# Batch 0's second MLP layer in seven products, with the weight sums made in its first layer

## The chip, the cores and the metric

The kernel runs on 1 core of one Trainium2 chip. The metric is the device time of one execution in microseconds (us); the number given for a kernel is the median of its runs. The engines are TensorE (PE; its weight loads are listed as PEld), VectorE (DVE), ScalarE (ACT), GpSimd (POOL) and the queue SyncE (SP), on which nearly all loads and stores are issued. Each engine works through its own instructions in order. A difference under about 1% can't be told from no change with the runs used here.

## The reference

Retention (a linear attention with decay) feeds a mixer with a low-rank step over the tokens and an MLP over the channels:

```python
state = gamma * state + k[t] ⊗ v[t];  x[t] = scale * q[t] @ state      # 4 batches, 8 heads, 768 tokens, 64 wide
u  = x + ((x.T @ U) @ V).T                                             # U 768x32, V 32x768
ch = np.maximum(u @ w_ch1, 0.0) @ w_ch2                                # w_ch1 512x2048, w_ch2 2048x512
out = u + ch                                                           # (4, 768, 512), float32
```

## The kernel before, in words

All matrix products run in bfloat16, with sums in PSUM in float32. Tokens are cut into 6 chunks of 128. The program is a list of slots: `weave(main, side)` walks over the main slots of a batch and, ahead of slot i, puts out the work that `put(side, i, f)` has filed there. What is left over for slots past the last one comes at the end, with no main work between. The text of the program thus fixes the order on every engine; an engine never leaves its own order, and waits only for data and for buffers.

A batch b takes two stages, and the attention of batch b+1 is filed as side work in them:

* **First MLP layer** (`mlp1`, `mlp1_two`): 32 slots, one for each of 16 blocks m of 128 hidden channels and each half hf of the tokens (384). A slot is 4 matmuls `bk<-uT,w1b` of 384 columns, and a Relu by ACT or DVE (`evict`) into `gT`. `n1` = 32 is the first slot of the second layer.
* **Second MLP layer**. Batch 0 uses `mlp2`: 48 slots, each 2 matmuls `bk<-w2b,gT` of 512 columns; the first slot of a token chunk also makes `Vb @ Ps` (the low-rank part of `u`) in the same PSUM bank, and the last adds `x` on DVE and stores the chunk. Batches 1 to 3 use `product`: `gT` and `w2b` are cut in quarters and seven quarter products (named "4", "5", "1", "2", "3", "7", "6" in the order in which they run) give what eight would. That is 3 token chunk pairs x 7 products x 2 halves = 42 slots of 4 matmuls of 256 columns. `after` adds each product to the result: ACT copies some products out of PSUM (`s`, `c`), POOL adds those copies, DVE adds others straight from PSUM. The low-rank part is then made apart, by `mix_r`, ahead of the products: a matmul of 512 columns and a DVE add into `res`.

The seven products need sums of quarters. `g_sums(b, n)` makes those of `gT` on DVE, five instructions of 768 elements for each of four groups n; it is filed in the first layer where its blocks are done, the last group at slot n1. `w2_sum(i)` makes those of `w2b` on DVE: three into `w2s`, two in place into `w2b`, each of 2048 elements in a partition. Batches 1 to 3 use the same sums, and before the change they are made once, in batch 1's first layer, at slots 5, 8, 11, 14 and 17.

The side work of one chunk of the next batch's attention: `ret_in` (POOL makes `kd` and `qd` from the loaded float32 chunks), `ret_T` (PE turns them into a bank, ACT or DVE copies them out as `qkT`; from batch 2 on by DMA), `ret_S` (the scores, 64-row matmuls, and two DVE instructions that mask them into `a`), `ret_O` (output, running sum and state). After the last chunk come `mix_P`, `mix_n` and `mix_u`, which make `uT` for the next first layer. `at`, `S_at`, `O_at` and `lead` hold the slots.

w1 comes in six loads and w2 in four, all issued by POOL within the first 30 us; a load of w2 holds four blocks m. `w2_quads` cuts w2 into b11, b12 (blocks 0 to 7, left and right) and b21, b22 (blocks 8 to 15).

Of the kernel before, what the change touches and what calls it, by code (L numbers as in the profile page):

```python
# [47 lines left out]
def kernel(  # L48
# [58 lines left out]
    def mm_bank(who="main"):  # L107
        if use[who] is None:
            who = "main"
        b = use[who][n_use[who] % len(use[who])]  # L110
        n_use[who] += 1
        taken[b] = n_bank[0]
        return bank(b)

    def matmul(o, l, r, cols, **kw):
        nc.tensor.matmul(o, l, r, **kw)  # L116
        bal.mm(cols)
# [407 lines left out]
    def res_of(b, j):  # L525
        if (b, j) not in res:
            res[b, j] = resp.tile([P, DM], fp32, tag="res", name=f"res_{b}_{j}")
        return res[b, j]
# [32 lines left out]
        for m, o in zip(ms, g):  # L561
            evict(gTs[b][:, m, ts(hf, HS)], o, HS, relu=True)

    chp = {}

    def mlp2(b, j, part, of):

        if part == 0:
            chp[b, j] = mm_bank()
            matmul(chp[b, j], Vb[:, ts(j, P)], Ps[b], DM, start=True, stop=False)  # L570
        ch = chp[b, j]
        for m in range(part * NM // of, (part + 1) * NM // of):
            matmul(ch, gTs[b][:, m, ts(j, P)], w2b[:, m], DM, start=False, stop=(m == NM - 1))
        if part == of - 1:
            o = res_of(b, j)
            nc.vector.tensor_tensor(o, chp.pop((b, j)), xs[b, j], op=ALU.add)
            bal.book("V", 0.69)
            nc.sync.dma_start(out=out[b, ts(j, P)], in_=o)
# [6 lines left out]
    def w2_quads():  # L585
        left, right = ds(0, HN), ds(HN, HN)
        return w2b[:, lo, left], w2b[:, lo, right], w2b[:, hi, left], w2b[:, hi, right]

    def w2_sum(i):
        b11, b12, b21, b22 = w2_quads()  # L590
        o, x, y, op = ((w2s[:, 0], b11, b22, ALU.add), (w2s[:, 1], b11, b12, ALU.add),
                       (w2s[:, 2], b21, b22, ALU.add), (b12, b12, b22, ALU.subtract),
                       (b21, b21, b11, ALU.subtract))[i]
        nc.vector.tensor_tensor(o, x, y, op=op)
        bal.book("V", 1.2)

    gss = {}

# [108 lines left out]
    def mlp2_slots(b, of=8):  # L707
        if b == 0:
            return [lambda j=j, i=i: mlp2(b, j, i, of) for j in range(NCK) for i in range(of)]
# [17 lines left out]
    def put(side, i, f):  # L727
        side.setdefault(int(i), []).append(f)
# [52 lines left out]
    for f, *args in (  # L781
# [10 lines left out]
        (qd, 2, 0, V), (turn_q, 2, 1), (keep, 3, 0), (load_w1, 0, 256), (load_w1, 256, 256),  # L792
# [13 lines left out]
        (evict_u, 1, 3, A), (evict_u, 1, 2, V), (load_w1, 512, 256),  # L806
        (load_w1, 768, 256),
    ):
        f(*args)

# [1 line left out]
    for b in range(B):  # L812
        nxt = b + 1 < B
        slots = mlp1_slots(b)
        n1 = len(slots)
        side = {}
        set_banks([0, 1, 2, SA, SB, OB])
        if b == 0:
            taken.update({i: n for n, i in enumerate((1, 2, 0, OB, SA, SB, TP))})
            set_banks([1, 2, 0, OB, SA, SB, TP])  # L820
            slots[:4] = [lambda: mlp1_two(0, (0, 1), 0), lambda: None,
                         lambda: mlp1_two(0, (0, 1), 1), lambda: None]
            for i, s in ((1, 2), (2, 3)):
                put(side, i, lambda s=s: load_w1(512 * s, 512))
            for s in range(4):
                put(side, 4 + s, lambda s=s: load_w2(s))
            for c, nm in ((0, "kq"), (1, "kq"), (2, "kq"), (0, "v"), (3, "kq"), (1, "v"), (4, "kq"),
                          (2, "v"), (3, "v"), (5, "kq"), (4, "v"), (5, "v")):
                put(side, 14, lambda c=c, nm=nm: load_chunk(1, c, nm))
            at, lead, mix_at = [n1 + 7 + 5 * c for c in range(NCK)], 4, n1 + 38  # L830
            S_at = {(0, 1): n1 + 14, (2, 3): n1 + 24, (4,): n1 + 30, (5,): n1 + 35}
            O_at = [n1 + i for i in (19, 22, 29, 32, 35, 38)]
        if b == 1:
            slots[:2] = [lambda: mlp1_two(1, (0, HM), 0), lambda: None]
            for j in range(NCK):
                if not by_token(1, j):
                    put(side, 6 + 3 * j, lambda j=j: mix_r(1, j))
            for i in range(5):
                put(side, 5 + 3 * i, lambda i=i: w2_sum(i))
        if b:  # L840
            for n, i in enumerate((13, 17, 25, n1)):
                put(side, i, lambda n=n: g_sums(b, n))
            banks = [0, 1, 2, TP] if nxt else [0, 1, 2, TP, SA, SB, OB, ST]
            put(side, n1, lambda: free_from(banks))
        if b and nxt:
            set_banks([0, 1, 2])
            at, lead, mix_at = [10 + 4 * c for c in range(NCK)], 5, n1 + 21
            S_at = {(0, 1): 27, (2,): 36, (3,): 40, (4,): 44, (5,): 48}
            O_at = [31, 34, 41, 45, 49, 53]
        if nxt:  # L850
            ret_side(b + 1, at, lead, S_at, O_at, side)
            if b == 0:
                put(side, n1, lambda: set_banks([0, 1], [2]))
            put(side, mix_at, lambda: use.update(mix=[2, SA, SB, OB] if b == 0 else [SA, SB, OB]))
# [35 lines left out]
```

## Time and profile before

| | us |
|---|---|
| median of 3 runs | 226.21 |
| lowest, highest | 225.68, 227.8 |
| the profiled execution | 227.9 |
| its span in the profile | 226.1 |
| PE busy in the span | 215.3 |
| DVE, ACT, POOL busy | 127.8, 124.3, 92.4 |

A row of the timeline gives start and length in us, engine, line, operation, output<-inputs, shapes and how many instructions were merged; in brackets the idle time ahead of it and what ended that. A row of the windows gives, for each engine, busy time and number of instructions in a stretch, then the granted clock of TensorE (1.00 is full), and the DMA's share and rate. A row on a tile gives shortest, median and longest duration in ns.

### The profile page before, as it was taken

What the parts mean: (1) busy time and instruction counts of PE and PEld (TensorE: products, weight loads), DVE (VectorE), ACT (ScalarE), POOL (GpSimd) and SP (SyncE); (2) the same over time, 40 slices, a digit from 0 to 9 for tenths busy, and PEclk for the clock granted to TensorE, in tenths of its full rate; (3) what the DMA queues carried; (4) which work ended last, traced back from release to release, by engine and by line L of the source; (5) the groups of instructions that cost most, each with busy time, mean ns of one, the idle gap of its engine ahead of it and who ended that gap; (6) DMA issues with size and microseconds to landing.
All of it is one profiled execution on the core that took longest, in us unless ns stands there. A gap on an engine that the chain in (4) does not pass through costs nothing.

```text
span 226.1 us, 4887 instructions
## 1 busy us (share of the span) xinstructions
PE 215.3 (95%) x1927; PEld 144.5 (64%) x1927; DVE 127.8 (57%) x249; ACT 124.3 (55%) x256; POOL 92.4 (41%) x110
## 2 busy tenths in 40 slices
PE   7998999999999999994999999999999999999991
PEld 2466656655656465652788776557887865568881
DVE  8497630003777466999884831668983632555213
ACT  3377757751355376764356546777544747772220
POOL 6856920047643512641143279513606230006550
PEclk9999999999999999998899999999999999999999
DMA  6998999999999999996599268979630651000222
GB/s 172 244 263 176 167 182 205 197 215 229 203 251 233 229 202 216 181 183 93 111 231 236 83 142 209 209 132 173 73 117 2 162 94 71 0 3 0 93 97 93
DMA packets 100774, 34.89 MB, mean 154 GB/s; under 512 B 87152, under 2 KB 97808, under 8 KB 100752
## 3 DMA queue, kind: packets, MB, share of 16 engines
q1 hardware_dynamic: 94640, 30.29, 66.0%
q0 software_dynamic: 6112, 4.29, 12.9%
q8 instruction: 15, 0.25, 0.5%
q14 instruction: 7, 0.06, 0.1%
HBM read 27.46 MB, written 6.29 MB: 149 GB/s over the span
## 4 chain that ended last, share of the span: by engine, by line
PE 66%; issue 11%; SPq 7%; POOL 7%; DMA 5%; DVE 1%; ACT 1%; POOLq 0%; DVEq 0%; ACTq 0%
PE bk L116 64%; DMA v_n<-in_v_dram 3%; POOL res L661 3%; POOL s L661 3%; SPq L136 2%; SPq L166 2%; SPq L288 2%; DMA q_n<-in_q_dram 2%; PE bk L424 1%; DVE res L661 1%; POOL qd L262 1%; ACT st L299 1%; POOL kd L257 0%; POOLq L885 0%; ACT kT L299 0%
## 5 line engine op out<-in xcount | busy, mean ns | idle before, releaser
L116 PE MATMUL bk<-uT,w1b 128*128 128x384 bf16 x512 | 85.9, 328 | 0.4 <-DVE res L661 0.4
L121 ACT ACTIVATE gT<-bk 128x384 bf16<-128x384 f32 x124 | 60.6, 490 | 30.2 <-PE bk L116 30.2
L116 PEld LDWEIGHTS <-w1b 128*128 128x128 bf16 x512 | 50.0, 98 | 33.6 <-issue 1.2
L116 PEld LDWEIGHTS <-gT 128*128 128x128 bf16 x392 | 36.9, 99 | 14.3 <-issue 1.2
L116 PE MATMUL bk<-w2b,gT 128*128 128x256 bf16 (+1 forms) x240 | 44.6, 319 | 0.0
L661 POOL TENSOR_TENSOR s<-s,s 128x256 f32<-128x256 f32 x18 | 13.1, 729 | 65.0 <-ACT s L657 65.0
L257 POOL TENSOR_TENSOR kd<-k_n,Gk 128x512 bf16<-128x512 f32 x18 | 20.1, 1117 | 47.5 <-ACT gT L121 18.9
L608 DVE TENSOR_TENSOR gs<-gT 128x768 bf16<-128x768 bf16 x36 | 22.9, 674 | 21.6 <-ACT gT L121 21.3
L446 DVE TENSOR_TENSOR a<-bk,mask 128x512 bf16<-128x512 f32 x36 | 22.8, 684 | 4.5 <-PE bk L116 4.4
L661 DVE TENSOR_TENSOR res<-bk,res 128x256 f32<-128x256 f32 x28 | 10.8, 420 | 21.6 <-PE bk L116 17.1
L116 PEld LDWEIGHTS <-gs 128*128 128x128 bf16 x216 | 20.5, 98 | 3.0
L262 POOL TENSOR_TENSOR qd<-q_n,Gq 128x512 bf16<-128x512 f32 x18 | 19.9, 1105 | 6.2 <-DMA qkT<-qd 3.8
L116 PE MATMUL bk<-w2b,gs 128*128 128x256 bf16 x144 | 19.7, 273 | 0.0
L463 ACT ACTIVATE x<-bk 128x512 bf16<-128x512 f32 x18 | 10.7, 595 | 15.0 <-PE bk L116 13.1
L116 PE MATMUL bk<-w2s,gT 128*128 128x256 bf16 (+1 forms) x152 | 18.5, 267 | 0.0
L657 ACT ACTIVATE s<-bk 128x256 f32<-128x256 f32 x27 | 10.1, 381 | 15.2 <-PE bk L116 14.9
L125 DVE COPY qkT<-bk 128x1024 bf16<-128x1024 bf16 x3 | 2.1, 692 | 23.9 <-PE bk L424 23.9
L268 ACT ACTIVATE vb<-v_n 128x512 bf16<-128x512 f32 x18 | 11.2, 623 | 5.8 <-DMA v_n<-in_v_dram 5.8
L661 POOL TENSOR_TENSOR res<-res,s 128x256 f32<-128x256 f32 x18 | 13.0, 724 | 1.4
L533 DVE TENSOR_TENSOR res<-bk,x 128x512 f32<-128x512 f32 x18 | 11.6, 685 | 3.4 <-PE bk L116 3.4
L116 PE MATMUL bk<-vb,a 128*128 128x64 bf16 (+1 forms) x208 | 10.3, 195 | 3.1 <-DVE a L446 3.1
L538 ACT ACTIVATE x<-res 128x512 bf16<-128x512 f32 x15 | 9.1, 627 | 6.3 <-DVE res L533 6.2
(99 smaller groups left out, 234.5 us busy)
## 6 DMA issues: line engine op xcount, KB each, us to landing
out_dram<-res SPq DMA_DIRECT2D x23, 256.0 KB, 2.4
k_n<-in_k_dram SPq DMA_DIRECT2D x22, 256.0 KB, 5.0
v_n<-in_v_dram SPq DMA_DIRECT2D x22, 256.0 KB, 4.8
q_n<-in_q_dram SPq DMA_DIRECT2D x18, 256.0 KB, 5.1
w2b<-in_moe_w_ch_dram POOLq DMA_DIRECT2D x4, 512.0 KB, 15.2
in<-in_q_dram SPq DMA_DIRECT2D x3, 512.0 KB, 6.3
w1b<-in_moe_w_ch_dram POOLq DMA_DIRECT2D x4, 256.0 KB, 5.7
w1b<-in_moe_w_ch_dram POOLq DMA_DIRECT2D x2, 512.0 KB, 9.1
```

The lines of the kernel that those rows point to most:

```text
L116: nc.tensor.matmul(o, l, r, **kw)
L121: nc.scalar.activation(o, i, AF.Relu if relu else AF.Copy)
L257: eng.tensor_tensor(kd, k_n, Gk[:, c].unsqueeze(2).to_broadcast([P, H, D]), op=ALU.mult)
L262: eng.tensor_tensor(qd, rc[b, c]["q_n"], Gq[:, c].unsqueeze(2).to_broadcast([P, H, D]), op=ALU.mult)
L268: nc.scalar.activation(vb, rc[b, c]["v_n"], AF.Copy)
L446: nc.vector.tensor_tensor(r["a"][:, e], r["s"][e].rearrange("p (n t) -> p n t", n=NP), mask4, op=ALU.mult)
L463: nc.scalar.activation(x_of(b, c), o, AF.Copy)
L533: nc.vector.tensor_tensor(res_of(b, j), h, xs[b, j], op=ALU.add)
L538: nc.scalar.activation(xs[b, j], res[b, j], AF.Copy)
L608: nc.vector.tensor_tensor(o, x, y, op=op)
L657: nc.scalar.activation(t[nm], o, AF.Copy)
L661: eng.tensor_tensor(o, x, y, op=op)
```

## The change

Batch 0 uses the seven products too. So `mlp2` goes; `mix_r` makes batch 0's low-rank part in its first layer (slots 4, 6, 13, 15, 21, 23); `g_sums` runs for batch 0 as well (slots 9, 17, 25 and n1). The sums of w2 move from batch 1's first layer to batch 0's and are cut in two halves h (four blocks m of each side, 1024 elements): the five of half 0 are filed at slot 19 and go to POOL, those of half 1 at slot n1-2, four on DVE and one on POOL. For the halves to be there, w1 and w2 are loaded in pairs of blocks (first of the upper and the lower half, then the next), and batch 0's first layer takes its blocks in the order 0, 1, 8, 9, 2, 3, 10, 11 and so on. Batch 1's scores come one chunk at a time, with new slots for its attention; its last pieces (`mix_n`, `mix_u`) get slots 41 to 47 behind n1, where the last main slot is n1+41. The PSUM banks of batch 0's second layer are 0, 1, 2 for the products.

```diff
-    def w2_sum(i):
-        b11, b12, b21, b22 = w2_quads()
-        o, x, y, op = ((w2s[:, 0], b11, b22, ALU.add), (w2s[:, 1], b11, b12, ALU.add),
-                       (w2s[:, 2], b21, b22, ALU.add), (b12, b12, b22, ALU.subtract),
-                       (b21, b21, b11, ALU.subtract))[i]
-        nc.vector.tensor_tensor(o, x, y, op=op)
-        bal.book("V", 1.2)
+    def w2_sum(i, h, eng):
+        b11, b12, b21, b22 = (x[:, ts(h, HM // 2)] for x in w2_quads())
+        z = w2s[:, :, ts(h, HM // 2)]
+        o, x, y, op = ((z[:, 2], b21, b22, ALU.add), (b21, b21, b11, ALU.subtract),
+                       (z[:, 0], b11, b22, ALU.add), (z[:, 1], b11, b12, ALU.add),
+                       (b12, b12, b22, ALU.subtract))[i]
+        eng.tensor_tensor(o, x, y, op=op)
...
         if b == 0:
-            return [lambda m=m, hf=hf: mlp1(b, m, hf) for m in range(NM) for hf in (0, 1)]
+            ms = [m + x for m in range(0, HM, 2) for x in (0, 1, HM, HM + 1)]
+            return [lambda m=m, hf=hf: mlp1(b, m, hf) for m in ms for hf in (0, 1)]
...
-            at, lead, mix_at = [n1 + 7 + 5 * c for c in range(NCK)], 4, n1 + 38
-            S_at = {(0, 1): n1 + 14, (2, 3): n1 + 24, (4,): n1 + 30, (5,): n1 + 35}
-            O_at = [n1 + i for i in (19, 22, 29, 32, 35, 38)]
+            for j, i in enumerate((4, 6, 13, 15, 21, 23)):
+                put(side, i, lambda j=j: mix_r(0, j))
+            for i in range(5):
+                put(side, 19, lambda i=i: w2_sum(i, 0, nc.gpsimd))
+                put(side, n1 - 2, lambda i=i: w2_sum(i, 1, nc.gpsimd if i == 2 else nc.vector))
+            for n, i in enumerate((9, 17, 25, n1)):
+                put(side, i, lambda n=n: g_sums(b, n))
+            at, lead, mix_at = [n1 + i for i in (7, 11, 16, 21, 26, 30)], 4, n1 + 36
+            S_at = {(c,): n1 + i for c, i in enumerate((10, 14, 19, 24, 29, 33))}
+            O_at = [n1 + i for i in (14, 18, 23, 28, 33, 36)]
         if b == 1:
...
-            for i in range(5):
-                put(side, 5 + 3 * i, lambda i=i: w2_sum(i))
```

The first place is POOL between the loads of w2 and the second chunk of batch 1's attention (`w2s`, `w2b`: the sums of w2; `kd`, `qd`: that attention's inputs; `s`, `res`: the adds of `after`). Before:

```order
L157 DMA w2b<-in_moe_w_ch_dram 128x4x512 x4
L257 TENSOR_TENSOR kd_0_885<-k_n_0_730,Gk 128x512
L262 TENSOR_TENSOR qd_0_887<-q_n_0_733,Gq 128x512
L257 TENSOR_TENSOR kd_1_913<-k_n_1_736,Gk 128x512
L262 TENSOR_TENSOR qd_1_915<-q_n_1_738,Gq 128x512
```

The same place on POOL after the change:

```order
L578 TENSOR_TENSOR w2s<-w2b 128x1024
L578 TENSOR_TENSOR w2b<-w2b 128x4x256
L578 TENSOR_TENSOR w2s<-w2b 128x1024 x2
L578 TENSOR_TENSOR w2b<-w2b 128x4x256
L578 TENSOR_TENSOR w2s<-w2b 128x1024
L257 TENSOR_TENSOR kd_0_948<-k_n_0_748,Gk 128x512
L262 TENSOR_TENSOR qd_0_950<-q_n_0_751,Gq 128x512
L646 TENSOR_TENSOR s_956<-s_941,s_956 128x256
L646 TENSOR_TENSOR res_0_669<-res_0_669,s_956 128x256
L646 TENSOR_TENSOR s_969<-s_969,s_956 128x256
L646 TENSOR_TENSOR res_3_795<-res_3_795,s_969 128x256
L257 TENSOR_TENSOR kd_1_977<-k_n_1_754,Gk 128x512
```

Six sums now stand ahead of the first `kd`, and four adds of product results ahead of the second.

The second place is DVE at the change from batch 0's first layer to its second (`gs`, `gT`: `g_sums`). Before, two Relus of the first layer's start are followed at once by the second layer:

```order
L123 TENSOR_SCALAR gT_639<-bk_53_641 128x384
L123 TENSOR_SCALAR gT_639<-bk_55_655 128x384
L125 COPY qkT_0_906<-bk_85_897 128x1024
L576 TENSOR_TENSOR res_0_910<-bk_84_877,x_0_395 128x512
L125 COPY qkT_1_936<-bk_87_927 128x1024
```

After, from the last `mix_r` of the first layer on:

```order
L533 TENSOR_TENSOR res_5_861<-bk_80_859,x_5_580 128x512
L593 TENSOR_TENSOR gs_708<-gT_639 128x768 x3
L593 TENSOR_TENSOR gT_639<-gT_639 128x2x384 x2
L578 TENSOR_TENSOR w2s<-w2b 128x1024
L578 TENSOR_TENSOR w2b<-w2b 128x4x256
L578 TENSOR_TENSOR w2s<-w2b 128x1024
L578 TENSOR_TENSOR w2b<-w2b 128x4x256
L593 TENSOR_TENSOR gs_708<-gT_639 128x768 x3
L593 TENSOR_TENSOR gT_639<-gT_639 128x2x384 x2
L646 TENSOR_TENSOR res_0_669<-bk_91_943,res_0_669 128x256
```

The second of these w2 sums writes the lower half of b21, which the second half of the first product ("4", the second slot of the second layer) reads.

The third place is DVE in batch 1's first layer. Before:

```order
L594 TENSOR_TENSOR w2s<-w2b 128x2048
L533 TENSOR_TENSOR res_2_1479<-bk_137_1477,x_2_1165 128x512
L608 TENSOR_TENSOR gs_1487<-gT_1376 128x768 x3
L608 TENSOR_TENSOR gT_1376<-gT_1376 128x2x384 x2
L594 TENSOR_TENSOR w2b<-w2b 128x8x256 x2
L608 TENSOR_TENSOR gs_1487<-gT_1376 128x768 x3
L608 TENSOR_TENSOR gT_1376<-gT_1376 128x2x384 x2
L608 TENSOR_TENSOR gs_1487<-gT_1376 128x768 x3
L608 TENSOR_TENSOR gT_1376<-gT_1376 128x2x384 x2
L446 TENSOR_TENSOR a_0_1643<-bk_153_1623,mask 128x512
```

After:

```order
L533 TENSOR_TENSOR res_2_1639<-bk_146_1637,x_2_1245 128x512
L593 TENSOR_TENSOR gs_1647<-gT_1539 128x768 x3
L593 TENSOR_TENSOR gT_1539<-gT_1539 128x2x384 x2
L593 TENSOR_TENSOR gs_1647<-gT_1539 128x768 x3
L593 TENSOR_TENSOR gT_1539<-gT_1539 128x2x384 x2
L593 TENSOR_TENSOR gs_1647<-gT_1539 128x768 x3
L593 TENSOR_TENSOR gT_1539<-gT_1539 128x2x384 x2
L446 TENSOR_TENSOR a_0_1801<-bk_162_1781,mask 128x512
```

The w2 sums are gone from there; ahead of the first mask `a` of batch 2 stand only the sums of `gT`.

More of the change, by code (lines that the diff above doesn't have):

```diff
@@ L562, in mlp1_two @@
             evict(gTs[b][:, m, ts(hf, HS)], o, HS, relu=True)
[L564 to L578, printed above, removed]
     HM, HN, HJ = NM // 2, DM // 2, NCK // 2
@@ L705, in mlp1_slots, with mlp2_slots @@
                 + [(m, hf) for m in late for hf in (0, 1)]]
-    def mlp2_slots(b, of=8):
-        if b == 0:
-            return [lambda j=j, i=i: mlp2(b, j, i, of) for j in range(NCK) for i in range(of)]
+    def mlp2_slots(b):
         slots = [lambda i=i, nm=nm, p=p: product(b, i, nm, p, 2)
@@ L791 @@
         (intra, 0), (keep, 2, 1), (scores, 3), (evict_x, 0, A), (sums, 1), (inter, 1), (intra, 1),
-        (qd, 2, 0, V), (turn_q, 2, 1), (keep, 3, 0), (load_w1, 0, 256), (load_w1, 256, 256),
+        (qd, 2, 0, V), (turn_q, 2, 1), (keep, 3, 0), (load_w1, 0, 256), (load_w1, DH // 2, 256),
         (turn_k, 4), (turn_q, 2, 0), (keep, 3, 1), (evict_x, 1, V), (evict_k, 4, V), (state, 1, A),
@@ L805 @@
         (evict_u, 0, 2, V), (evict_u, 0, 3, V), (high, 1, 1), (evict_u, 1, 1, V), (high, 1, 3),
-        (evict_u, 1, 3, A), (evict_u, 1, 2, V), (load_w1, 512, 256),
-        (load_w1, 768, 256),
+        (evict_u, 1, 3, A), (evict_u, 1, 2, V), (load_w1, 256, 256),
+        (load_w1, DH // 2 + 256, 256),
     ):
@@ L822 @@
                          lambda: mlp1_two(0, (0, 1), 1), lambda: None]
[L823 to L826, printed above, removed]
+            for i, s in ((1, 512), (2, DH // 2 + 512)):
+                put(side, i, lambda s=s: load_w1(s, 512))
+            for n, s in enumerate((0, 2, 1, 3)):
+                put(side, 4 + n, lambda s=s: load_w2(s))
             for c, nm in ((0, "kq"), (1, "kq"), (2, "kq"), (0, "v"), (3, "kq"), (1, "v"), (4, "kq"),
```

13 lines of the change are left out of this document (7 added, 6 removed).

## The prediction

> **What bounds the kernel now.** I read the page's head first, then the windows by stage, the waits of PE, and the timeline around the one long wait.
>
> ```profile
> span 226.1 us, 4887 instructions
> PE 215.3 (95%) x1927; PEld 144.5 (64%) x1927; DVE 127.8 (57%) x249; ACT 124.3 (55%) x256; POOL 92.4 (41%) x110
> ```
>
> PE is busy for 95% of the span, so time is won by giving PE less to do or by ending its waits, and lost by new waits. The windows are batch 0's first and second layer, then batch 1's.
>
> ```profile
> 27.48:48.21 20.73, 20.73 (x130) 12.42 (x127) 2.80 (x6) 14.68 (x33) 2.15 (x3) 1.00 1.21 198
> 48.21:81.57 33.36, 33.36 (x313) 18.68 (x312) 18.55 (x29) 13.61 (x24) 18.63 (x18) 1.00 1.14 235
> 81.57:108.38 26.81, 23.73 (x160) 14.13 (x159) 23.73 (x32) 16.50 (x34) 8.41 (x6) 0.96 0.97 155
> 108.38:135.39 27.01, 26.58 (x294) 21.52 (x292) 17.34 (x35) 14.14 (x30) 10.78 (x16) 0.98 0.76 164
> ```
>
> In batch 0's stages PE (first number behind the length) never rests. DVE (third) has only 2.80 us of work in the first of them, POOL (fifth) 2.15. In batch 1's first layer PE lacks 3.08 us, and the clock is below full there:
>
> ```profile
> PE bk L116 <- DVE a L446: 3.1, 1, 3.1
> 102.70 0.49 PE L116 MATMUL bk<-uT,w1b 128*128 128x384 bf16 x2
> 106.27 0.61 PE L116 MATMUL bk<-vb,a 128*128 128x64 bf16 x8 [3.08 <-DVE a L446]
> 106.30:107.30 1.00, 1.00 (x13) 0.95 (x14) 0.52 (x1) 0.38 (x1) 0.00 (x0) 0.50 0.41 79
> 109.30:110.30 1.00, 1.00 (x18) 0.90 (x17) 1.00 (x3) 0.28 (x1) 0.00 (x0) 0.89 0.66 131
> ```
>
> PE waits for a mask of batch 2 and then runs at half clock until about 109.5 (0.89 of the last row's us means 0.2 us at half): 3.2 us at half lose 1.6. The two matmuls at 102.70 fill until 103.0, so the place costs 3.25 + 1.6 = 4.85 us. DVE is late for this reason:
>
> ```profile
> 95.97 2.06 DVE L594 TENSOR_TENSOR w2b<-w2b 128x2048 bf16<-128x2048 bf16 x1
> 97.96 1.48 DVE L608 TENSOR_TENSOR gs<-gT 128x768 bf16<-128x768 bf16 x3
> 100.30 3.19 DVE L608 TENSOR_TENSOR gs<-gT 128x768 bf16<-128x768 bf16 x3
> 104.34 2.47 DVE L446 TENSOR_TENSOR a<-bk,mask 128x512 bf16<-128x512 f32 x4
> ```
>
> The w2 sums push the sums of gT back, and these the masks. Batch 2, which has the same slots without w2 sums, is the control:
>
> ```profile
> 152.00 1.02 DVE L608 TENSOR_TENSOR gT<-gT 128x768 bf16<-128x768 bf16 x2
> 152.94 2.48 DVE L446 TENSOR_TENSOR a<-bk,mask 128x512 bf16<-128x512 f32 x4
> 155.55 0.40 PE L116 MATMUL bk<-vb,a 128*128 128x64 bf16 x8
> ```
>
> There the masks begin at 152.94, the first two are ready 1.2 us later, and PE takes them up at 155.55 without a wait.
>
> **The change, part by part.** Gains first; the prices of PE:
>
> ```profile
> 52.70 1.89 PE L116 MATMUL bk<-w2b,gT 128*128 128x512 bf16 x8
> 54.88 1.03 PE L116 MATMUL bk<-w2b,gT 128*128 128x512 bf16 x4
> 55.84 0.62 PE L116 MATMUL bk<-qkT 64*128 64x128 bf16 x16
> 56.39 0.39 PE L116 MATMUL bk<-w2b,gT 128*128 128x512 bf16 x1
> 202.88 1.04 PE L116 MATMUL bk<-w2b,gT 128*128 128x256 bf16 x8
> 205.50 1.04 PE L116 MATMUL bk<-w2b,gs 128*128 128x256 bf16 x8
> ```
>
> *Products.* Eight matmuls of 512 columns take 1.89 us with the drain of the last (0.39, as the single one shows), so 0.215 each. Between 202.88 and 205.50 stand 24 of 256 columns: 0.109 each. 96 x 0.215 = 20.65 go, 168 x 0.109 = 18.3 come: -2.35 us. The six low-rank matmuls only move: 1.3 us into the first layer, out of the second.
>
> *The wait in batch 1.* With the w2 sums gone its first layer is like batch 2's: -4.85 us. If POOL's work stretches the sums of gT there as it did at 100.30, about 1 us of wait could stay.
>
> *Scores by chunk.* The four 512-column matmuls at 54.88 end their columns at 55.74 and the scores begin at 55.84; sixteen in eight pairs take 0.55 until 56.39, where eight pairs of 128 columns, at half the price of 256, are 0.44. A switch to 64-row matmuls and back so costs 0.2. There are six calls where there were four: +0.4.
>
> *The w2 sums at their new place.* This term decides. No row shows a sum of 1024 bfloat16 elements on POOL; these are the nearest, with those of DVE:
>
> ```profile
> L257 POOL TENSOR_TENSOR kd<-k_n,Gk x18: 1032/1042/1982, 48.5 to 153.2; 128x512 bf16<-128x512 f32 x18
> L661 POOL TENSOR_TENSOR res<-res,s x18: 722/724/727, 112.8 to 219.9; 128x256 f32<-128x256 f32 x18
> L301 POOL CAST vb<-v_n x2: 396/396/397, 23.0 to 23.4; 128x256 bf16<-128x256 f32 x2
> L608 DVE TENSOR_TENSOR gs<-gT x36: 545/554/1399, 90.8 to 204.1; 128x768 bf16<-128x768 bf16 x36
> L594 DVE TENSOR_TENSOR w2s<-w2b x3: 1214/1215/1215, 83.5 to 88.7; 128x2048 bf16<-128x2048 bf16 x3
> ```
>
> Scaled to 1024: two of `kd` 2.08 us, four adds 2.90, four casts, which read one input, 1.58. I take 2.08, since `kd` reads two inputs, writes bfloat16 and is nearest in size. [...] For DVE, between 0.55 and 1.21: 0.6 for 1024.
>
> POOL and DVE also keep each other out when both read two operands from SBUF:
>
> ```profile
> 90.74 1.04 POOL L262 TENSOR_TENSOR qd<-q_n,Gq 128x512 bf16<-128x512 f32 x1
> 90.83 1.37 DVE L608 TENSOR_TENSOR gs<-gT 128x768 bf16<-128x768 bf16 x1
> 94.84 1.21 DVE L594 TENSOR_TENSOR w2b<-w2b 128x2048 bf16<-128x2048 bf16 x1
> 95.06 1.90 POOL L262 TENSOR_TENSOR qd<-q_n,Gq 128x512 bf16<-128x512 f32 x1 [1.49 <-DMA qkT<-qd]
> ```
>
> `gs` (0.55 alone) ends 0.42 after `qd` does; `qd` (1.04 alone) ends 0.91 after the DVE instruction does, and the next on DVE, quoted at 95.97, waits for it in turn. So they take turns.
>
> ```profile
> L157 POOL DMA_DIRECT2D w2b<-in_moe_w_ch_dram x2: 780/785/790, 26.6 to 27.4; - x2
> DMA to landing us min/median/max: 12.2/13.0/13.8
> ```
>
> The second load of w2, now blocks 8 to 11, lands at 27.4 + 13.8 = 41.2, and POOL starts its sums, whatever their slot. DVE's third group of gT sums has its data once slot 23 is done: 27.48 + 96 x 0.162 + 1.3 = 44.3, and the copy into gT, so about 45. From then POOL has five or so sums left, `kd` and `qd`; DVE has five sums of gT, then the w2 sums, of which the second (b21) is what PE needs. In turns, b21 is ready after all of POOL's eight and seven of DVE's: 41.2 + 6 x 2.08 + 2 x 1.0 + 5 x 0.42 + 2 x 0.6 = 59.0. PE reaches the second half of product "4" at 48.21 + 1.3 + 4 x 0.109 = 49.9. It waits 9.1 us (6.1 to 14.0 by the other prices); nothing covers it, since all of PE's later work is queued behind. The sums that follow are ready in time for "5" and "1".
>
> *The clock after it.* A wait of 3.1 us lost 1.6 us: +1.6. [...]
>
> *Batch 1's attention behind POOL's adds.*
>
> ```profile
> L657 ACT ACTIVATE s<-bk 128x256 f32<-128x256 f32 x27 | 10.1, 381 | 15.2 <-PE bk L116 14.9
> ```
>
> `kd`, `qd` of chunk 1 come after four adds: from the end of product "5", 0.2 for the drain and 0.38 for ACT's copy, then 4 x 0.72 and 2 x 1.04, 5.5 us. PE has seven half products (3.05), a transposition (8 x 0.055) and one chunk's scores (0.5) in between, 4.0, and half a us more while the clock is low: +1.0; at chunk 4, again behind adds, about +0.5. Between 0 and 4.
>
> *The end of the stage.* The last `mix_n` and all `mix_u` now follow the last product with no main slot between, so that each waits for its bank to be emptied: +0.5 (0 to 1.5).
>
> *At no cost:*
>
> ```profile
> L533 DVE TENSOR_TENSOR res<-bk,x 128x512 f32<-128x512 f32 x18 | 11.6, 685 | 3.4 <-PE bk L116 3.4
> L152 POOL DMA_DIRECT2D w1b<-in_moe_w_ch_dram x6: 746/754/815, 21.0 to 25.9; - x6
> DMA to landing us min/median/max: 3.8/6.1/10.0
> ```
>
> Six `mix_r` adds (0.685 each) and two groups of gT sums (ten of 0.55) are 9.6 us on DVE in batch 0's first layer, where it is idle for 17.9. The loads keep their sizes and places in the queue: the last of w1 is there at 25.9 + 10.0 = 35.9, and the new order needs it at slot 20, 27.48 + 80 x 0.162 + 0.9 = 41.3.
>
> Sum: -2.35 - 4.85 + 0.4 + 9.1 + 1.6 + 1.5 + 0.5 = +5.9. The profiled execution took 227.9 (226.1 and 1.8 around), 1.7 above the median, and would take 233.8; on the median of 226.21 that is 232.1 us.
>
> **The rivals.**
>
> *A. Two-byte sums run twice as fast on POOL*, 1.04 each. Then b21 is ready at 52.8 and PE waits 2.9, with half the loss of clock: 226.2 - 6.8 + 2.9 + 0.8 + 2.0 = 225.1. Against it: no row of POOL shows a price by bytes.
>
> *B. No turns:* DVE gets through while POOL is at one sum. b21 is then in time, but `qd` of chunk 0 still ends no earlier than 41.2 + 12.5 + 2.0 = 55.7, and PE reaches its transposition, six half products of 0.437 after 49.9, at 52.5: wait 3.2, clock 0.8, so 226.2 - 6.8 + 3.2 + 0.8 + 2.0 = 225.4. The rows at 90.83 and 95.06 speak against it.
>
> *C. Faster: no wait comes at all.* The price per sum decides: under 0.56 us, six sums end in time for b21 at 49.9. Then 226.2 - 6.8 + 1.0 = 220.4. Only the idle POOL in this stage speaks for it.
>
> *D. Sums at the price of the float32 adds*, 2.90: +4.9, 237.0.
>
> **How the numbers follow.** The forecast's case 0.58 (its own range, 1.58 to 2.4 for a sum, 229.1 to 234.0), A 0.16, B 0.10, C 0.08, D 0.08. The range from 224.0 to 235.0 leaves out C, D and the fast end of A and B. Faster by over 1% (below 223.9): C, 0.05 of A and 0.04 of B, 0.17. Within 1%, about what a measurement of this kernel can tell from no change: most of A and B, 0.18. Slower: the rest, 0.65.
>
> **What would show it.** In the profile after: POOL's L578 rows near 2.1 us with DVE's between them, one wait of PE of 6 to 11 us near 50 us on DVE's w2b and half clock behind it, no wait on a mask in batch 1's first layer, smaller waits for `qd` in batch 0's second. The prediction is wrong if L578 on POOL is near 1 us, or if DVE's sums near 45 to 55 us are not stretched to POOL's ends.

## The result and the profile after

The changed kernel is slower: 237.4 us, the median of 4 runs (237.0 to 237.78), against 226.9 (225.68 to 227.8, 4 runs) for the kernel before, measured beside it; the ratio is 1.0495, 95% interval 1.0439 to 1.0551. The profiled executions took 237.78 and 227.9, so that +9.9 stands against the +5.9 of the sum. Some executions of a kernel are 2 us or more longer, at a lower mean granted clock (0.992 or less against 0.995 or more in the 13 of the kernel before that are counted under batch 1 below); the ratios leave out the longest of them and need not be those of the medians. The direction was right; the time, 232.1, and the upper end of the range, 235.0, were too low.

The head of the page after: PE has 0.7 us more work, and its share has fallen from 95% to 92%.

```profile
span 235.8 us, 5098 instructions
PE 216.0 (92%) x1997; PEld 152.1 (64%) x1999; DVE 148.4 (63%) x280; ACT 129.5 (55%) x268; POOL 115.4 (49%) x131
```

The windows after, for batch 0's first and second layer, then batch 1's (PE, weight loads, DVE, ACT, POOL, granted clock):

```profile
27.62:49.80 22.18, 22.18 (x137) 13.10 (x134) 16.76 (x25) 14.83 (x33) 10.22 (x7) 1.00 1.18 198
49.80:93.86 44.06, 33.77 (x377) 26.32 (x377) 31.62 (x47) 18.59 (x36) 34.41 (x36) 0.88 0.84 173
93.86:116.64 22.78, 22.72 (x159) 13.64 (x159) 14.38 (x24) 16.15 (x35) 7.39 (x8) 1.00 0.91 167
116.64:143.93 27.29, 25.75 (x290) 20.74 (x288) 18.27 (x36) 13.96 (x30) 10.60 (x16) 1.00 0.86 172
```

Nearly all that is lost lies in the second row. That stage took 32.98 us before, from the first w2 matmul at 48.59 to 81.57:

```profile
48.59:81.57 32.98, 32.98 (x311) 18.48 (x310) 18.55 (x29) 13.39 (x23) 18.52 (x18) 1.00 1.15 237
```

Now it takes 44.06, with a PE that works for 33.77 of them, part of that at half clock. Its busiest engine is POOL with 34.41 us. The third row is the gain that was expected: no wait is left in batch 1's first layer, 22.78 where 26.81 stood. The fourth gives part of it back. It ends at the first w1 matmul of batch 2; before, that matmul came at 134.14 (the prediction's row runs on to 135.39), so this layer took 25.76 us before and takes 27.29 now.

The waits of PE after:

```profile
PE bk L116 <- DVE w2b L578: 8.5, 1, 8.5
PE bk L116 <- DMA uT<-x: 0.9, 1, 0.9
PE bk L424 <- POOL qd L262: 0.9, 2, 0.7
PE bk L116 <- ACT s L642: 0.6, 1, 0.6
PE bk L116 <- ACT uT L121: 0.6, 1, 0.6
```

The wait for b21 (`w2b` of L578) is the one forecast. This view counts from the drain of the last matmul; from the end of its columns each wait is about 0.2 longer, 8.7 for the first. The sums go by the latter.

POOL and DVE ahead of that wait, first POOL:

```profile
41.67 2.12 POOL L578 TENSOR_TENSOR w2s<-w2b 128x1024 bf16<-128x1024 bf16 x1 [11.88 <-DMA w2b<-in_moe_w_ch_dram]
43.87 2.12 POOL L578 TENSOR_TENSOR w2b<-w2b 128x1024 bf16<-128x1024 bf16 x1
45.95 4.82 POOL L578 TENSOR_TENSOR w2s<-w2b 128x1024 bf16<-128x1024 bf16 x2
50.85 2.31 POOL L578 TENSOR_TENSOR w2b<-w2b 128x1024 bf16<-128x1024 bf16 x1
```

And DVE:

```profile
44.76 6.43 DVE L593 TENSOR_TENSOR gs<-gT 128x768 bf16<-128x768 bf16 x3
51.11 4.85 DVE L593 TENSOR_TENSOR gT<-gT 128x768 bf16<-128x768 bf16 x2
...
57.44 1.41 DVE L578 TENSOR_TENSOR w2b<-w2b 128x1024 bf16<-128x1024 bf16 x1
```

A sum takes POOL 2.12 us alone and about 2.4 in turns. DVE's sums of `gT`, 0.55 each alone, take 2.1 to 2.4 (6.43 for three, 4.85 for two): each waits out one of POOL. DVE's adds with one operand in a PSUM bank are not held up so: `res<-bk,x` at 42.63 and at 44.15 lie inside POOL's first two sums (41.67 and 43.87) and take 0.69 each, as elsewhere. b21 ends at 58.85 (57.44 + 1.41), and PE goes on at 58.91; 59.0 was worked out.

### The profile page after: what moved, and what is told of

Read it like the earlier page. It is cut to its first block, busy times and chain, and to the rows that moved or that the text cites. A ratio compares the mean times of both kernels' runs of the same rounds, so it can differ in the third digit from the quotient of the medians.

```text
span 235.8 us, 5098 instructions
## 1 busy us (share of the span) xinstructions
PE 216.0 (92%) x1997; PEld 152.1 (64%) x1999; DVE 148.4 (63%) x280; ACT 129.5 (55%) x268; POOL 115.4 (49%) x131
## 4 chain that ended last, share of the span: by engine, by line
PE 70%; DVE 8%; DMA 5%; POOL 5%; SPq 4%; ACT 3%; issue 3%; POOLq 0%; DVEq 0%; ACTq 0%
PE bk L116 69%; DVE gs L593 3%; DMA v_n<-in_v_dram 3%; SPq L166 2%; SPq L136 2%; POOL s L646 2%; DMA uT<-x 2%; DVE gT L593 1%; POOL res L646 1%; DVE w2b L578 1%; DVE w2s L578 1%; POOL kd L257 1%; POOL qd L262 1%; PE bk L424 1%; DVE res L646 1%
## 5 line engine op out<-in xcount | busy, mean ns | idle before, releaser
L646 POOL TENSOR_TENSOR s<-s,s 128x256 f32<-128x256 f32 x24 | 17.7, 738 | 70.0 <-ACT s L642 66.2
L593 DVE TENSOR_TENSOR gs<-gT 128x768 bf16<-128x768 bf16 x48 | 32.2, 710 | 21.1 <-ACT gT L121 20.6
L116 PE MATMUL bk<-w2b,gT 128*128 128x256 bf16 x192 | 26.9, 276 | 9.1 <-DVE w2b L578 8.5
L116 PEld LDWEIGHTS <-gs 128*128 128x128 bf16 x288 | 28.3, 102 | 4.9
L116 PE MATMUL bk<-w2b,gs 128*128 128x256 bf16 x192 | 27.6, 282 | 0.0
L116 PE MATMUL bk<-w2s,gT 128*128 128x256 bf16 (+1 forms) x200 | 24.8, 269 | 0.0
L593 DVE TENSOR_TENSOR gT<-gT 128x768 bf16<-128x768 bf16 x32 | 21.8, 722 | 0.0
L578 POOL TENSOR_TENSOR w2s<-w2b 128x1024 bf16<-128x1024 bf16 x4 | 9.4, 2351 | 11.9 <-DMA w2b<-in_moe_w_ch_dram 11.9
L116 PE MATMUL bk<-w2s,gs 128*128 128x256 bf16 x96 | 13.7, 285 | 0.0
L482 DVE TENSOR_TENSOR state<-bk,bmask 128x512 bf16<-128x512 f32 x15 | 10.3, 689 | 4.2 <-PE bk L116 4.2
```

Of the source, the lines that this page charges most:

```text
L482: nc.vector.tensor_tensor(sb, ps.rearrange("p (n t) -> p n t", n=NP), bmask4, op=ALU.mult)
L578: eng.tensor_tensor(o, x, y, op=op)
L646: eng.tensor_tensor(o, x, y, op=op)
```

## The experiments

### No sums on POOL

All ten half sums go to DVE, at the same slots.

```diff
-                put(side, 19, lambda i=i: w2_sum(i, 0, nc.gpsimd))
-                put(side, n1 - 2, lambda i=i: w2_sum(i, 1, nc.gpsimd if i == 2 else nc.vector))
+                put(side, 19, lambda i=i: w2_sum(i, 0, nc.vector))
+                put(side, n1 - 2, lambda i=i: w2_sum(i, 1, nc.vector))
```

> All ten half sums of w2 on DVE, at the same slots, none on POOL. Theory (turns): POOL's sums and DVE's sums of gT shut each other out, and PE waits 8.7 us for b21 behind them and then loses 3.0 us at half clock; without POOL's sums b21 is ready near 49.5 us, the wait and the half clock go, about 0.7 us stays for the last group of gT sums, and the span is 235.8 - 8.7 - 3.0 + 0.7, about 225, the time about 226.5. Rival (the seven products don't pay in this stage, wherever the sums are made): the waits come back for other adds of POOL and DVE, and the time stays over 232.

Measured: 230.34 us (228.96 to 231.04, 4 runs), span 227.7, ratio to the kernel before 1.0202 (1.0118 to 1.0286). PE's waits, then the stage's window:

```profile
PE bk L424 <- POOL qd L262: 3.0, 2, 2.1
PE bk L116 <- DVE gs L593: 2.0, 1, 2.0
PE bk L116 <- DVE w2b L578: 0.3, 1, 0.3
```

```profile
49.54:86.82 37.28, 31.06 (x377) 24.67 (x377) 24.83 (x43) 19.43 (x37) 28.02 (x33) 1.00 0.99 205
```

The wait for b21 is down to 0.3 and the clock stays full: the span is 8.1 us shorter. POOL's sums, which the rows above show in turns with DVE, thus made the long wait. But the stage is still 4.3 us longer than the 32.98 of before, though PE has less to do in it. Two waits that stood behind the first have come up: DVE's last group of `gT`, and `qd` of POOL.

### Shorter turns

The sums of the third group of `gT` are left out in batch 0 (zeros stand in their place; this part of the computation is missing).

```diff
-            for n, i in enumerate((9, 17, 25, n1)):
+            put(side, 10, lambda: nc.vector.memset(gss[0][:, :, ds(4, 2)], 0.0))
+            for n, i in ((0, 9), (1, 17), (3, n1)):
```

> The third of batch 0's four groups of gT sums is left out (zeros stand in its place), the w2 sums stay where they are. Theory (turns): DVE is free for its w2 sums when the last load of w2 lands near 48.2 us; each still waits for one POOL sum, so b21 is ready near 53.3 and PE waits about 3 us instead of 8.7. Rival (POOL's queue alone is late, DVE does not wait for it): b21 is ready near 49.5 with no wait, and PE waits for qd of chunk 0, ready near 56, instead.

Measured in one run: 234.29 us, span 232.3.

```profile
PE bk L116 <- DVE gs L593: 4.0, 1, 4.0
PE bk L116 <- DVE w2b L578: 2.7, 1, 2.7
```

With five partners in the turns gone, b21 comes at 52.8, and PE waits 2.7 for it instead of 8.5, as turns demand. But then it waits 4.0 for the last group of `gT`, which stands behind DVE's own sums of w2, and these are in turns with POOL. Of the 5.8 us won at the first wait 3.5 are left in the span.

### Full clock through the wait

38 idle matmuls of 512 columns stand in the wait, so that PE does not rest.

```diff
+            def fill(n):
+                w = bank(ST)
+                for _ in range(n):
+                    nc.tensor.matmul(w, idle[:, :P], idle, start=True, stop=True)
+            put(side, n1 + 1, lambda: fill(38))
```

> 38 matmuls of 512 columns on zeros ahead of the second half of product 4, 8.2 us that lie inside the wait. Theory: the half clock from 54.6 to 64.9 cost PE 3.0 us behind the wait; with PE kept at work the clock stays at 1.0 and the span falls from 235.8 to about 232.8. Rival: behind the wait PE is held by DVE's sums and POOL's adds anyway, and the span falls by less than 1.

Measured in one run: 237.51 us, span 235.5, within the 235.0 to 235.8 of the changed kernel's four runs. The clock in the changed kernel (PE's busy time, granted clock, DMA), then in this variant (all engines):

```profile
54.65:58.90 4.25, 0.00 (x0) 0.50 1.09 216
58.90:64.90 6.00, 5.99 (x33) 0.50 1.29 220
64.90:67.00 2.10, 2.10 (x26) 1.00 1.30 218
```

```profile
58.75:67.80 9.05, 6.35 (x67) 5.07 (x67) 6.16 (x11) 3.08 (x7) 6.20 (x8) 1.00 0.98 191
67.85:71.20 3.35, 3.35 (x31) 2.31 (x29) 1.56 (x4) 1.03 (x2) 3.35 (x4) 0.50 0.42 116
```

The idle matmuls keep the clock full past 58.75, and almost nothing is won by it: PE now runs into `qd` of the second chunk, and waits for it until nearly the same moment, 67.03 against 67.45.

```profile
67.03 0.40 PE L424 MATMUL bk<-ident,qd 128*128 128x128 bf16 x4 [2.14 <-POOL qd L262]
```

That wait is 0.24 in the changed kernel. Up to this matmul, keeping the clock won 0.4 us: POOL's chain to `qd` sets the time there, and the half clock in the changed kernel lay beside it. Behind it the clock falls after all, from 67.85 to 71.2, so the length of the whole span does not show the price of the clock by itself.

### Kernel before, without the sums of w2

In the kernel before, the five sums are left out (w2s is set to zero, the in-place sums are missing). This is the most that moving them could bring to batches 1 to 3.

```diff
+            put(side, 10, lambda: nc.vector.memset(w2s, 0.0))
...
-            for i in range(5):
-                put(side, 5 + 3 * i, lambda i=i: w2_sum(i))
```

> The kernel before, with the five sums of w2 left out of batch 1's first layer (w2s is zero, b12 and b21 stay as loaded). Theory: they alone cause the wait of 3.1 us for a mask and the half clock behind it, so the first layer of batch 1 loses 4.9 us of length. Rival 1: all of it reaches the end, span 221.3. Rival 2: the queue of loads and transposes sets the start of batch 2's first layer, and 1 to 2 us are given back there, span 222.5 to 223.

Measured: 224.78 us (224.09 to 227.38, 10 runs), ratio 0.9941 (0.9891 to 0.9991), which is 1.3 us. The span of the profiled execution, 222.7, is 3.4 less than that of the profiled one before; why these two differ is said below, under batch 1. Batch 1's two layers:

```profile
81.65:104.21 22.56, 22.56 (x160) 13.64 (x159) 15.28 (x26) 15.80 (x33) 7.20 (x6) 1.00 1.15 173
104.21:130.73 26.52, 25.59 (x290) 20.78 (x288) 17.59 (x34) 13.94 (x30) 9.52 (x14) 1.00 0.90 181
```

The first layer is 4.25 us shorter. The second took 25.76 up to the first w1 matmul of batch 2; 0.55 of half clock goes there too (1.1 us at half, 108.38 to 109.5), so it should be 25.2, and it takes 26.5. Where that goes, PE, then DVE and ACT, then SyncE show:

```profile
128.11 1.03 PE L116 MATMUL bk<-w2b,gT 128*128 128x256 bf16 x8 [0.93 <-ACT s L657]
```

```profile
125.82 1.30 DVE L533 TENSOR_TENSOR res<-bk,x 128x512 f32<-128x512 f32 x2 [1.12 <-DMA out_dram<-res]
126.55 1.24 ACT L538 ACTIVATE x<-res 128x512 bf16<-128x512 f32 x2 [0.91 <-DVE res L533]
```

```profile
110.71 0.58 SPq L136 DMA_DIRECT2D k_n<-in_k_dram  x1
...
119.23 0.89 SPq L136 DMA_DIRECT2D v_n<-in_v_dram  x1
120.22 1.06 SPq L689 DMA_DIRECT2D out_dram<-res  x1
```

Nine loads of batch 3 are issued from 110.71 to 120.1, and a store of a result only behind them. DVE waits for the landing of a store (it writes a buffer that the store still reads), ACT for that DVE instruction, and PE, 2.3 us later, for ACT's copy `s`, which stands behind.

### The same sums, made early without seven products

Two variants of the kernel before, with the function computed in full: three of the five sums (into w2s) are made in batch 0, in halves, on DVE, and only the two in-place sums stay in batch 1.

```diff
+            for i in range(3):
+                put(side, 24, lambda i=i: w2_sum(i, 0))
+                put(side, n1 + 4 + 9 * i, lambda i=i: w2_sum(i, 1))
...
-            for i in range(5):
-                put(side, 5 + 3 * i, lambda i=i: w2_sum(i))
+            for i in (3, 4):
+                put(side, 5 + 3 * (i - 3), lambda i=i: w2_sum(i))
```

> The kernel before (eight blocks a chunk for batch 0's second layer), with the three w2 sums that have a place of their own made by DVE in halves in batch 0's stages, and the two that write into w2b left in batch 1's first layer, at slots 5 and 8. Theory: the wait for a mask of batch 2 and the half clock behind it go as in the kernel with no w2 sums; DVE's four extra us in batch 0's second layer lie in its slack; span about 223, time about 224.8. Rival: in batch 0's second layer DVE and POOL shut each other out and PE waits there for 1 us or more: span 224 or over.

The second has the nine loads of batch 3 later as well:

```diff
-            for c, i in enumerate((31, 36, 41)):
+            for c, i in enumerate((46, 50, 54)):
```

> The same, and in batch 1's second layer the loads of batch 3 are filed at slots 46, 50, 54 instead of 31, 36, 41, so that the first two stores of batch 1's results stand ahead of them in SP's queue. Theory: about 1.0 us of the gain is given back because the stores wait behind nine loads, their result buffers come free late, DVE's next low-rank add waits for the store, and PE at the end for ACT's copies behind it; with the stores first that wait goes and the span falls by about 1.0 against the kernel without this edit. Rival: SP's queue is full in any case and the wait moves to the transposes of uT: no gain.

Measured: 225.33 us (224.43 to 228.55, 10 runs), ratio 0.9969 (0.9925 to 1.0014), and 226.88 (225.64 to 230.3, 10 runs), ratio 1.0023 (0.9966 to 1.008). Neither can be told from the kernel before. In both profiled executions batch 1's first layer is as short as without any sums, 22.56. That of the first variant took 228.55 us, the longest of its ten, and is read no further but for its transposing copies, below. The second variant's second layer, and what PE waits for:

```profile
104.01:131.96 27.95, 25.71 (x290) 20.73 (x288) 18.65 (x37) 13.88 (x30) 11.94 (x17) 1.00 0.86 171
```

```profile
PE bk L116 <- DMA uT<-x: 2.2, 1, 2.2
```

The later loads let the stores go, and now stand ahead of the transposing copies of `uT` instead: 2.4 of the 4.25 us are given back at that place (from the end of the columns at 129.55 to 131.96).

### kd and qd ahead of the adds

On top of the variant without sums on POOL, `kd` and `qd` of each chunk are made five slots earlier, ahead of POOL's adds.

```diff
-            at, lead, mix_at = [n1 + i for i in (7, 11, 16, 21, 26, 30)], 4, n1 + 36
+            at, lead, mix_at = [n1 + i for i in (7, 11, 16, 21, 26, 30)], 9, n1 + 36
```

> All w2 sums on DVE as in e1, and batch 1's kd and qd filed 9 slots ahead of their transpositions instead of 4, so that on POOL those of chunk 1 and of chunk 4 stand ahead of the adds of product results. Theory: the waits of 2.3 and 1.1 us for qd in batch 0's second layer come from these adds standing first; they go, and the span falls from 227.7 to about 224.4. Rival: POOL is full or waits for the loads, and the waits stay within 1 us of what they were.

Measured: 230.69 us (229.81 to 231.7, 4 runs), ratio 1.0204 (1.0112 to 1.0295): no gain over the 230.34 without that step. PE's waits, and POOL:

```profile
PE bk L116 <- DVE gs L593: 3.6, 1, 3.6
PE bk L116 <- ACT s L642: 1.8, 1, 1.8
```

```profile
48.48 1.49 POOL L257 TENSOR_TENSOR kd<-k_n,Gk 128x512 bf16<-128x512 f32 x1 [18.83 <-ACT gT L121]
...
52.83 1.48 POOL L262 TENSOR_TENSOR qd<-q_n,Gq 128x512 bf16<-128x512 f32 x1
```

The waits for `qd` in this stage are gone, but four instead of two of these now run in turns with DVE's sums (1.48 each, 1.04 alone), and the wait for DVE grows from 2.0 to 3.6; behind it the clock is not full either (eight matmuls of 256 columns at 55.79 take 1.91 us, at 59.28 again 1.04; 0.95 as the mean of 49.5 to 87, where the run without that step had 1.00). That takes up what `qd` gave. At the end of batch 1's second layer 1.8 us come up on a copy of ACT, where there were 0.2.

### All of it together

The sums on DVE, the last two of half 1 behind the last group of `gT`, `lead` 8, the attention of batch 1 two to five slots earlier and its last pieces four.

```diff
-                put(side, n1 - 2, lambda i=i: w2_sum(i, 1, nc.gpsimd if i == 2 else nc.vector))
+                put(side, n1 - 2 if i < 3 else n1 + 1, lambda i=i: w2_sum(i, 1, nc.vector))
...
-            at, lead, mix_at = [n1 + i for i in (7, 11, 16, 21, 26, 30)], 4, n1 + 36
+            at, lead, mix_at = [n1 + i for i in (5, 9, 13, 18, 22, 26)], 8, n1 + 32
...
```

> All w2 sums on DVE, the last two of half 1 after the last group of gT sums, kd and qd 8 slots ahead, and batch 1's attention and last pieces four slots earlier, so that main slots stand between the last pieces. Theory: the seven products are worth 2.35 us of PE in batch 0 once nothing waits; the waits of 2.2 for the last group, 3.4 for qd and 1.8 at the stage's end fall to about 1 in all, span about 221.5, below the kernel before. Rival: the added work on DVE, ACT and POOL keeps this stage longer than with eight blocks, and the span stays at 224 or over.

Measured: 229.46 us (227.68 to 232.04, 4 runs), ratio 1.0126 (1.0032 to 1.022). In the profiled execution (232.04 us, the longest of the four) the waits at the end of the stage are gone but for 0.2, since the last pieces now lie between main slots, but three waits for DVE of 0.5, 1.5 and 3.2 us come ahead of them. The median is the lowest of the variants with seven products and all the sums in batch 0, though the intervals overlap, and it is still above the kernel before. The expected span of 221.5 did not come.

### The changed kernel without any sum of w2

The five sums are left out of the changed kernel (w2s is zero, the in-place sums are missing): what seven products in batch 0 cost if the sums are free.

```diff
-            for i in range(5):
-                put(side, 19, lambda i=i: w2_sum(i, 0, nc.gpsimd))
-                put(side, n1 - 2, lambda i=i: w2_sum(i, 1, nc.gpsimd if i == 2 else nc.vector))
+            put(side, 10, lambda: nc.vector.memset(w2s, 0.0))
```

> The changed kernel with none of the ten half sums of w2 (w2s set to zero once by DVE at slot 10 of batch 0's first layer, the in-place ones left out); the output is not the reference's. It is to tell apart what seven products in batch 0 cost by themselves from what the sums of w2 cost at their new place. Theory 1: all waits of batch 0's second layer in the changed kernel and in the variant with all sums on DVE (there 0.46 + 2.16 + 2.31 + 1.06) come from the sums, directly or by the turns with POOL. Then without sums only the 1.8 us at the end of the stage stay: batch 1's first layer starts at 49.6 + 29.7 + 1.8 = 81.1 us, and the span is about 222, the same as that of the kernel before without the sums (222.7). Theory 2: POOL's adds of product results ahead of kd and qd cost waits by themselves, with the loads of the second batch's k and q landing only at 48 us. Then 1.5 to 3.4 us of waits for qd stay, batch 1's first layer starts at 82.6 to 84.5, and the span is 223.5 to 225.5: seven products in batch 0 then gain nothing even when the sums are free.

Measured: 227.23 us (226.18 to 229.65, 10 runs), ratio 1.0029 (0.9975 to 1.0083), span 225.4: theory 2. The stage, PE's waits for `qd`, and POOL ahead of the longer one:

```profile
49.66:83.99 34.33, 30.72 (x378) 24.68 (x377) 22.66 (x41) 17.80 (x35) 26.85 (x32) 1.00 1.04 221
```

```profile
PE bk L424 <- POOL qd L262: 2.7, 2, 2.1
```

```profile
52.07 1.16 POOL L646 TENSOR_TENSOR s<-s,s 128x256 f32<-128x256 f32 x1 [1.72 <-ACT s L642]
...
55.48 1.04 POOL L257 TENSOR_TENSOR kd<-k_n,Gk 128x512 bf16<-128x512 f32 x1
56.48 1.04 POOL L262 TENSOR_TENSOR qd<-q_n,Gq 128x512 bf16<-128x512 f32 x1
```

Four adds and `kd` stand ahead of `qd`, 52.07 to 57.52, and PE takes it at 57.58, 2.1 us late. With the waits at the end of the stage this eats what seven products save. Against the kernel before without sums (222.7) the span is 2.7 longer, and by the two ratios (1.0029 and 0.9941) the time is about 2 us longer. The intervals of these ratios just overlap. So seven products in batch 0 gain nothing even with free sums, in this order of the work, and most likely lose.

### Loads on another queue

Does SyncE's queue itself set the end of batch 1's second layer, or the data that it moves? On top of the first variant with early sums, the nine loads of batch 3 are issued by POOL, then by ScalarE.

```diff
-        nc.sync.dma_start(out=n, in_=src[b, :, ts(c, P), :].rearrange("h p d -> p h d"))
+        eng = nc.gpsimd if b == B - 1 and c < 3 else nc.sync
+        eng.dma_start(out=n, in_=src[b, :, ts(c, P), :].rearrange("h p d -> p h d"))
```

> The kernel before with three of the five w2 sums made early (as in the variant before that gave 225.33), and with the nine loads of batch 3's first three chunks issued by POOL instead of by SyncE in batch 1. It is to show why the 4.2 us won in batch 1's first layer were given back in its second. Theory 1: SyncE's queue is the bound there; its issues stand back to back, some 1.1 us each from 100 to 150 us, and the stores of results and the transposed copies of uT stand behind these nine loads. With nine issues less ahead of them, PE's waits at the end of batch 1's second layer (3.03 at 129.9, or 2.4 on uT) shrink below 1 us, batch 2's first layer starts at 130.5 to 131.5 instead of 134.2, and the span is 222.5 to 224. Theory 2: what paces these issues is the moving of the data, whichever queue issues it; then the waits stay at 2 to 3 us and the span at 224.5 to 226.5. On POOL the issues take 0.8 us each, 7 us in all, ahead of adds of product results; a new wait of ACT or PE on these adds is possible.

> The same with the nine loads issued by ScalarE instead of POOL. Theory 1 (SyncE's queue is the bound): batch 2's first layer starts at 130.5 to 131.5, span 222.5 to 224, unless ScalarE's own work (the copies s, c and the Relus) is held up by the issues. Theory 2 (the moving of the data is the bound): as with SyncE, 224.5 to 226.5.

Measured: on POOL 228.01 us (224.03 to 231.82, 12 runs), ratio 0.9961 (0.991 to 1.0013), which is no difference. On ScalarE 229.22 (228.98 to 230.75, 6 runs), ratio 1.0146 (1.0091 to 1.0202). Its only long wait of batch 1, and ScalarE ahead of it; then the number and the median time from issue to landing of the copies of `qd` in it, and in the kernel before:

```profile
PE bk L116 <- ACT vb L269: 2.7, 1, 2.7
112.85 0.38 ACT L660 ACTIVATE s<-bk 128x256 f32<-128x256 f32 x1 [4.78 <-DMA qkT<-kd]
```

```profile
qkT<-qd SPq DMA_TRANSPOSE x12, 4.0
```

```profile
qkT<-qd SPq DMA_TRANSPOSE x12, 2.5
```

The spans do not tell the two theories apart. On POOL the four shortest executions have spans of 222.1 to 223.7, as theory 1 expected, but eight of the ten with the loads on SyncE lie there too (222.5 to 223.8), and the other eight on POOL are at 226.0 to 229.9. On ScalarE all spans, 227.2 to 228.9, lie above both expected ranges. There the waits at the end of the layer are nearly gone (0.5 is left, the one behind it that the kernel before had too), which speaks for the queue. But one at 113.8, on ScalarE, has come: its own work stops for 4.78 us, where the program has it issue three of the loads, and the stop is put down to transposing copies. These land 4.0 us after their issue, instead of 2.5 before and 3.1 in the first variant with early sums, where SyncE issues all of the loads. That would fit the moving of the data as the bound. Which of the two sets the end of the layer stays open.

## Why the prediction was wrong in the time

The steps as predicted, and as the trace after has them (spans; +9.7 between the two, where the profiled times differ by 9.9):

| step | predicted | measured |
|---|---|---|
| products, scores by chunk, low-rank part | -1.95 | -2.3 |
| wait for b21 | +9.1 | +8.7 |
| clock after it | +1.6 | +3.0 |
| waits for `qd` | +1.5 | +1.2 |
| end of the stage | +0.5 | +1.6 |
| batch 1's wait and clock, given back in part | -4.85 | -3.1 |
| end of the kernel | 0 | +0.5 |

With 0.1 that the first layer starts later, this is 9.7.

The largest term, the wait for b21, was right. The time failed on four other steps: the clock (1.4 us more than predicted), the end of the stage (1.1 more), the gain in batch 1 (1.75 less), and the way from the span to the median (1.3).

*Products and scores: right.* The first layer grew by 1.07 (22.18 against 21.11, 27.48 to 48.59). The second is 44.06; without 8.7, 3.0, 1.2 and 1.6 from this table 29.56 remain, 3.4 less than 32.98. Together -2.3.

*The wait for b21: right, in cause and size.* A sum at 2.12 against the 2.08 that I took from `kd`; the turns predicted b21 to 0.2 us, with some luck: POOL began 0.5 later than forecast (41.67), and the work from there took 0.6 less. The wait is 0.4 shorter, mainly because PE was ready for b21 only at 50.24, not at 49.9. The runs without POOL's sums and with shorter turns show the cause. Rival B (no turns) and rival A (half the price for two bytes) fell with these rows. The rows (a `gT` sum of 0.55 takes 2.1 to 2.4 beside POOL's) show that back-to-back sums on both sides come out as turns.

*The clock: size wrong.* PE went on at 58.91 and had full clock at 64.9: 6.0 us at half, 3.0 lost, where I carried over 1.6 from the one wait of before. The half clock lasted 10.25 us, and in the variant with idle matmuls 3.35. What sets its length is not shown; one wait of 3.1 us was too little to price the clock behind one of 8.7. And the step itself was no separate term: the variant that kept the clock through the wait was only 0.4 ahead at the second chunk's `qd`, because POOL's chain to it ran beside the slow stretch. Clock and `qd` together were 3.1 predicted and 4.2 measured.

*The end of the stage: size wrong.* From the last product group at 90.35 the columns end at 92.29 if nothing waits (0.43 for four of 256, 0.21 for one of 512, four times 0.32 for three of 128 and one of 384); the first w1 matmul comes at 93.86, so 1.6 us are lost.

```profile
90.35 0.60 PE L116 MATMUL bk<-w2s,gT 128*128 128x256 bf16 x4
...
92.23 0.33 PE L116 MATMUL bk<-ident,x 128*128 128x128 bf16 x3 [0.18 <-DVE res L533]
...
93.86 1.35 PE L116 MATMUL bk<-uT,w1b 128*128 128x384 bf16 x6 [0.55 <-ACT uT L121]
```

I named the mechanism (no main slot between) but priced one emptied bank, not the chain of DVE and ACT to the last `uT`. In the variant with these pieces four slots earlier the waits are gone, which bears this out, though that variant changes other things too.

*Batch 1: the step that failed in its reasoning.* I took the 4.85 us as kept, and as what any execution loses there. The wait and half clock did vanish, but the trace after shows 0.79 at 140.23 and 1.09 at 143.93, at the end of the second layer, where the kernel before had only 0.6, just behind that end. The prediction asked what a shorter wait triggers on PE, DVE and POOL, but not on SyncE. The variant of the kernel before without these sums loses part of its gain at the same place. So 3.1 of the 4.85 arrive between the two profiled executions. In the second variant with early sums, later loads moved the wait to `uT`, which bears out that loads and stores are in the way; whether the queue or the moving of the data sets it is open. Nor is it a fixed price: without sums on POOL the same layer takes 25.81 us, with 0.2 of wait at its end.

```profile
109.60:135.41 25.81, 25.59 (x290) 20.80 (x288) 17.59 (x34) 13.94 (x30) 9.53 (x14) 1.00 0.87 179
```

Moreover, the profiled execution of the kernel before, 227.9 us at a mean granted clock of 0.991, is one of its longer ones. Of its 13 executions measured beside the experiment without the sums, eight have a clock of 0.995 or more and a median of 225.4 us, five have 0.992 or less and 228.2. Without the sums of w2 eight of ten have 0.995 or more, with a median of 224.6. Between executions at such a clock, leaving the sums out thus gains 0.8 us, not 4.85. Why some executions lose clock and others not is not shown; two of the ten without sums lie at 0.992 or less too, so it is not this wait alone.

*From the span to the median: 1.3 us too low.* I took 1.7 us off, since the profiled execution before lay so far above its median. After, the four runs lie within 0.8 us, and the profiled one is only 0.4 above their median.

*The rest.* The last 0.5 us come behind PE's last matmul (4.71 us from there to the end before, 5.18 after, and 5.2 to 5.3 in the other seven-product variants). I did not follow it.

*What the sum could not show.* Taken term by term, removing the long wait should have brought about 225, as rivals A and B had it. The run without POOL's sums took 230.34 us, with a span of 227.7, and the one with no sums at all 227.23, with 225.4. Behind the long wait stood others that it hid: the last group of `gT`, `qd` behind POOL's adds, the end of the stage. In the changed kernel POOL is busy for 34.4 us of this stage where it had 18.5, DVE for 31.6 where it had 18.6, much of it in turns; the last three loads of w2 land at 41.6, 44.7 and 48.1 us and batch 1's first `k_n` at 48.4, so much of that work can't start sooner. Seven products save PE 2.3 us, and the work that they ask of these two around the change of layers delays it by more.

## What to carry to other kernels

Before you give a product scheme with fewer multiplications to a stage, count what its sums ask of the vector engines between the landing of their operands and their first use, adding both engines' times where they run in turns, as these sums with two operands in SBUF did here (0.55 us on DVE became 2.1 to 2.4 beside 2.12 on POOL). When a removed wait is put into a sum, look on every queue, the DMA queues too, for what is late next; an experiment that leaves the work out altogether shows with one edit about how much there is to gain. Compare several executions with several, with their clocks beside them: two profiles can differ by more than the change is worth. Price two delays that run beside each other (a slow clock and a late input) together.

## What the runs showed of the hardware

A POOL sum of 1024 bfloat16 elements takes 2.12 us, twice the 1.04 of `kd` with 512 float32 elements: no gain by two-byte operands shows in these rows. The same sum takes DVE 0.69 alone. Half clock lasted 10.25 us for a wait of 8.7, 6.0 of it behind the wait; a stretch in the variant with idle matmuls lasted 3.35, and in the kernel before 3.2 us of it lay behind a wait of 3.1. What starts and ends it is not shown. The transposing copies of `qd` land 2.5 us after their issue (median) in the kernel before, 3.1 and 2.5 in the two variants with three of the sums of w2 made early, and 4.0 when ScalarE issues loads beside them; what sets this is not shown.
